# Two second-layer value steps stand inside the dense stage: one in the gate rows, one in the query rows

## The chip, the cores and the metric

The kernel runs on one core of one Trainium2 chip. The metric is the device time of one execution in microseconds; the time of a kernel is the median of several executions. The engines are written as in the profile: PE is TensorE (PEld its weight loads), DVE is VectorE, ACT is ScalarE, SP is SyncE, whose queue issues every DMA of this kernel.

## What is computed

Decoding of one token for a batch of 4, through two layers that share their weights and caches. Each layer is an attention block over a cache of 4096 positions (32 query heads, 8 key heads of 128) and a gated feed-forward block (512 to 1792 and back). All inputs are bf16.

```python
def _A_ref(x, k_cache, v_cache, wq, wo):      # x (4, 1, 512), caches (4, 8, 4096, 128)
    q = (x @ wq) split into 32 heads of 128
    k, v = each of the 8 cached heads, for 4 query heads
    p = softmax(q @ k.T * 128 ** -0.5)
    return (p @ v, heads joined) @ wo

def _B_ref(x, w_gate, w_up, w_down):
    return (gelu(x @ w_gate) * (x @ w_up)) @ w_down

x = A_x
x = x + _A_ref(layernorm(x), ...)
x = x + _B_ref(layernorm(x), ...)
x = x + _A_ref(layernorm(x), ...)             # the second layer: same weights, same caches
x = x + _B_ref(layernorm(x), ...)
```

## The kernel before

The weights are loaded once and stay on the core. The key and value caches do not fit, so they are streamed, batch by batch, as tiles of 128 x 2048 bf16 (512 KB): 16 key tiles and 16 value tiles for one batch (8 heads, each in 2 halves). Because the second layer of batch b needs the same keys as its first layer, the kernel works on two things at once: the first layer of batch b + 1 and the second layer of batch b. The keys of a batch stay in their 16 tiles until both layers have used them. The values are streamed twice, once for each layer, through 7 buffers (`KV_BUFS`).

The order of all instructions is written out by hand, one stream for each engine, and each engine takes its own in program order. So does SP's queue: a load that has to wait for its buffer holds back every load behind it.

**A value step** (`Values.step`, L467) takes one value tile: 16 weight loads and 16 matmuls of 4 columns on PE (L481). After it, its buffer is free and the next value load is put on SP (`load_v`, L454 to L461). After every second head, that is every fourth step, DVE scales the finished pair by the inverse softmax sum and writes it as bf16 (L489); the last two heads of a batch are scaled one by one, after steps 14 and 16.

**Where the second layer's steps stand.** A batch has 16 of them. Four are done early, inside `attend`. The other 12 are handed to the next pass of the main loop (L679) as `fill`: `fill(n)` takes the next n steps, if any are left. In the pass of batch b the main loop runs

- `dense(b, 1, ...)` (L660), the feed-forward block of the first layer for one row: the end of the output projection, the sums for the layer norm (`ln_center`), the gate rows (`ffn_in`, L300, matmuls at L314), the up rows (L314 again), then `ln_rstd` (L183 to L202, ten small DVE instructions that make the inverse deviation), `gelu` (which first turns the gate rows on DVE, L215), `gate_up` (which turns the up rows and ends with `H_bf`, L340) and `down` (L347);
- the second layer's query: `ln_square`, `ln_center`, the query rows of the first group of heads (`q_rows`, L218, matmuls at L225), `ln_rstd`, `am` (L690), the turn of the query rows, `q_spread` (L236), `q_build` (L246 and L249, which writes `qb`);
- `attend` (L498), or `attend_last` (L618) for the last batch: scores of the second layer against the old keys (L383), after which the key tiles are free and the keys of the next batch are loaded into them (L365); in `attend_last` they take values instead. `fill` is passed on as `rest` and called with 1 after the scores of the first group and their `q_build`, with 1 again after their softmax exponentials, and with all that is left a little later. Then come the first layer's attention for the next batch, key tiles turned on DVE as they land (L372), scores, softmax, 16 first-layer value steps and the output projection.

`seen["hold"]` keeps first-layer value loads off SP from the start of `attend` until the key loads have been issued.

Before the change, the 12 steps stand like this: one after `out_proj_end`, one after `ln_center`, one between gate and up rows, two after the GELU is issued, one after `ln_square`, one after the second `ln_center`, two after `q_spread`, one after `q_build`, and two inside `attend` or `attend_last`. In the first pass of the loop there are none, since the second layer hasn't begun (`prev` is None), and the dense stage of all four rows at the end (L705) has none either.

## Time and profile before

| | |
|---|---|
| median of 7 runs | 317.94 us (316.8 to 320.58) |
| the profiled execution | 314.99 us |
| its span | 313.2 us, 8714 instructions |
| PE, PEld busy | 212.1 us (68%), 122.3 us (39%) |
| DVE, ACT busy | 171.4 us (55%), 28.9 us (9%) |
| DMA | 114.09 MB, 364 GB/s over the span |
| value steps: matmuls (L481, values from `v`) | 1920, 63.7 us |
| key turns on DVE (L372) | 64, 75.2 us |
| gate rows, up rows (L314) | 64 and 64 matmuls, 6.7 us each |

The span runs from the first to the last instruction of the program on the core; the execution's time includes what lies around it. Busy time is an average over stages with different limits, so what a change in one stage is worth has to be read from that stage: what ends its waits, and whether what comes after it is waiting too. In the timeline a line has the start, the duration, the engine, the line of the kernel, the operation and the tiles it writes and reads; a bracket at its end tells how long the engine stood idle before it, and what ended that. In the chain of waits a line has the start, the duration and the engine or transfer that the end of the program goes back to.

### The profile page before, as it was taken

Reading aid. Unit: us, or ns where it says so; the run is one execution under the profiler, and the core shown is the slowest. Engines: PE = TensorE matmul, PEld = TensorE weight load, DVE = VectorE, ACT = ScalarE, POOL = GpSimd, SP = SyncE. Lnnn points to the kernel's source line nnn. Section 1 sums busy time; section 2 is a strip of 40 time slices with the busy share of each in tenths; the row PEclk is TensorE's granted clock in tenths of the full one; section 3 lists DMA queues with packets and bytes.
Section 4 is the critical chain, followed back from the end, with each engine's and each line's share of the span. In section 5 each row is a group of like instructions: output and inputs, shape, how many; then the busy total and the mean of one; then the engine's idle time right before and its main releaser. Section 6 shows DMA issues by size and latency. Waiting matters only on the chain.

```text
span 313.2 us, 8714 instructions
## 1 busy us (share of the span) xinstructions
PE 212.1 (68%) x3844; PEld 122.3 (39%) x3844; DVE 171.4 (55%) x481; ACT 28.9 (9%) x70; POOL 0.7 (0%) x6
## 2 busy tenths in 40 slices
PE   1360485343577649989965469799762798997975
PEld 0010245211324124656441336564411465645654
DVE  5584761014247986455488934454799553545133
ACT  0002002000002020300010112000202040003000
POOL 0000000000000000000000000000000000000000
PEclk9999999999999555555765555556755555559555
DMA  7999999999949999999999999999999999999900
GB/s 256 368 413 397 409 409 406 356 371 393 384 151 337 402 407 408 386 393 408 395 397 409 409 406 383 396 404 362 363 413 407 410 406 359 397 406 408 378 5 3
DMA packets 35526, 114.09 MB, mean 364 GB/s; under 512 B 3224, under 2 KB 9120, under 8 KB 35488
## 3 DMA queue, kind: packets, MB, share of 16 engines
q1 hardware_dynamic: 35488, 113.53, 94.3%
q8 instruction: 30, 0.49, 0.6%
q14 instruction: 8, 0.07, 0.1%
HBM read 113.51 MB, written 0.00 MB: 362 GB/s over the span
## 4 chain that ended last, share of the span: by engine, by line
DMA 44%; PE 27%; DVE 15%; SPq 9%; issue 3%; ACT 2%; DVEq 0%; ACTq 0%
DMA kt<-in_A_k_cache_dram 22%; DMA v<-in_A_v_cache_dram 18%; PE ot L481 6%; PE sc L383 6%; DVE kt L372 5%; PE rows L280 3%; DMA wd_sb<-in_B_w_down_dram 3%; PE rows L314 3%; SPq L133 3%; SPq L127 3%; PE y L347 2%; PE rows L225 2%; PE x L429 1%; DVE pp L410 1%; DVE rows L215 1%
## 5 line engine op out<-in xcount | busy, mean ns | idle before, releaser
L481 PEld LDWEIGHTS <-v 128*128 128x128 bf16 x1920 | 59.8, 105 | 47.4 <-DMA v<-in_A_v_cache_dram 23.9
L372 DVE STREAM_TRANSPOSE kt<-kt 128x1024 f32<-128x1024 f32 x64 | 75.2, 1217 | 4.7 <-DMA kt<-in_A_k_cache_dram 4.5
L481 PE MATMUL ot<-pe,v 128*128 128x4 bf16 x1920 | 63.7, 167 | 18.4 <-DMA v<-in_A_v_cache_dram 17.1
L383 PE MATMUL sc<-kt,qb 128*32 128x512 bf16 x512 | 62.9, 545 | 15.6 <-DVE kt L372 12.4
L215 DVE STREAM_TRANSPOSE rows<-rows 128x512 f32<-128x512 f32 (+1 forms) x23 | 16.3, 707 | 38.9 <-PE rows L225 19.7
L383 PEld LDWEIGHTS <-qb 128*32 128x32 bf16 x512 | 17.3, 116 | 45.8 <-issue 29.9
L402 ACT ACTIVATE pp<-sc,nm 128x512 bf16<-128x512 f32 x16 | 11.0, 688 | 152.9 <-DVE junk L398 152.9
L429 PE MATMUL x<-pp,ident_bf 128*32 128x128 bf16 x256 | 9.1, 283 | 23.5 <-DVE pp L410 23.3
L489 DVE TENSOR_TENSOR OT_bf<-ot,rden 128x8 bf16<-128x8 f32 (+1 forms) x40 | 6.5, 164 | 33.4 <-PE ot L481 32.9
L280 PE MATMUL rows<-wo_sb,OT_bf 128*1 128x512 bf16 (+1 forms) x136 | 17.2, 611 | 7.4 <-DMA wo_sb<-in_A_wo_dram 6.3
L225 PE MATMUL rows<-wq_sb,xn_bf 128*1 128x512 bf16 (+1 forms) x160 | 18.5, 612 | 4.8 <-DMA wq_sb<-in_A_wq_dram 4.5
L429 PEld LDWEIGHTS <-ident_bf 128*32 128x32 bf16 x256 | 6.7, 121 | 29.6 <-issue 27.9
L389 DVE TENSOR_REDUCE m<-sc 128x1 f32<-128x512 f32 x16 | 10.8, 675 | 12.2 <-PE sc L383 12.2
L410 DVE STREAM_TRANSPOSE pp<-pp 128x512 bf16<-128x512 bf16 x16 | 11.2, 701 | 4.6 <-ACT pp L402 4.3
L432 ACT CAST pe<-x 128x512 bf16<-128x512 f32 x16 | 9.4, 585 | 21.5 <-PE x L429 21.5
L347 PE MATMUL y<-H_bf,wd_sb 128*128 128x1 bf16 (+1 forms) x280 | 8.6, 166 | 3.0 <-DMA wd_sb<-in_B_w_down_dram 2.3
L347 PEld LDWEIGHTS <-wd_sb 128*128 128x128 bf16 x280 | 8.1, 104 | 4.3 <-DMA wd_sb<-in_B_w_down_dram 3.3
L249 DVE TENSOR_TENSOR qb<-qe,amask 128x256 bf16<-128x256 f32 x16 | 6.8, 425 | 5.3 <-PE qe L246 5.3
L225 PEld LDWEIGHTS <-xn_bf 128*1 128x1 bf16 (+1 forms) x160 | 4.4, 110 | 13.2 <-issue 11.9
L246 PE MATMUL qe<-qm,t_bf 128*128 128x64 bf16 x16 | 3.4, 215 | 8.9 <-DVE qm L236 6.6
L415 PE MATMUL den<-zx,mean_f 128*128 128x16 f32 x32 | 8.9, 357 | 0.0
L420 DVE RECIPROCAL rden<-den 128x16 f32<-128x16 f32 x16 | 4.0, 250 | 8.8 <-PE den L415 8.3
(78 smaller groups left out, 124.8 us busy)
## 6 DMA issues: line engine op xcount, KB each, us to landing
v<-in_A_v_cache_dram SPq DMA_DIRECT2D x118, 512.0 KB, 8.3
kt<-in_A_k_cache_dram SPq DMA_DIRECT2D x64, 512.0 KB, 10.6
wq_sb<-in_A_wq_dram SPq DMA_DIRECT2D x2, 2048.0 KB, 7.8
wo_sb<-in_A_wo_dram SPq DMA_DIRECT2D x4, 1024.0 KB, 11.8
kt<-in_A_v_cache_dram SPq DMA_DIRECT2D x8, 512.0 KB, 8.7
wg_sb<-in_B_w_gate_dram SPq DMA_DIRECT2D x1, 1792.0 KB, 13.5
wu_sb<-in_B_w_up_dram SPq DMA_DIRECT2D x1, 1792.0 KB
wd_sb<-in_B_w_down_dram SPq DMA_DIRECT2D x1, 896.0 KB, 16.4
```

Of the source, the lines that this page charges most:

```text
L215: nc.vector.transpose(out=rows[:, :n], in_=rows[:, :n])
L225: nc.tensor.matmul(rows[j * QS:j * QS + nb, :], lhsT=xn_bf[:, k, bs], rhs=w, start=(k == 0), stop=(k == KD - 1))
L280: nc.tensor.matmul(rows[r0:r0 + lhsT.shape[-1], :], lhsT=lhsT, rhs=wo_sb[:, i, :], start=(start and n < QD), stop=(stop and n >= hp - QD))
L347: nc.tensor.matmul(y[:, k], lhsT=wd_sb[:, c, k * P:(k + 1) * P], rhs=H_bf[:, c, :], start=(c == 0 and k == 0), stop=(c == KF - 1), skip_gr ...
L372: nc.vector.transpose(out=words, in_=words)
L383: nc.tensor.matmul(sc[s * QS:(s + 1) * QS], lhsT=qb[:, w0:w0 + 2 * W], rhs=kt[:, :, be // 2, :, be % 2], start=(t == 0 and be == 0), stop= ...
L389: nc.vector.tensor_reduce(out=m[:], in_=sc.rearrange("p c j -> p (c j)"), axis=AX.X, op=ALU.max)
L402: nc.scalar.activation(out=pp[:], in_=sc[:], func=ACT.Exp, bias=nm[:, 0:1], scale=scale, accum_out=ls[:])
L410: nc.vector.transpose(out=flat, in_=flat)
L429: nc.tensor.matmul(x[a * QS:(a + 1) * QS, s], lhsT=ident_bf[:, s * QS:(s + 1) * QS], rhs=pT[:, a], start=True, stop=True, skip_group_check ...
L432: nc.scalar.copy(out=pe.rearrange("p s c h -> p (s c h)"), in_=x.rearrange("p s t c h -> p (s t c h)"))
L481: nc.tensor.matmul(self.ot[:, s % 2], lhsT=v[:, i, :], rhs=pe[:, s, c, :], start=(c == 0), stop=(c == C - 1), skip_group_check=True)
```

## The change

`ffn_in` and `q_rows` take one more argument, a function that is called halfway through their loop over the four parts of the contraction. The dense stage passes a value step for the gate rows (not for the up rows), the main loop one for the first group's query rows.

```diff
-    def q_rows(b0, nb, g):
+    def q_rows(b0, nb, g, half=lambda: None):
         bs = slice(b0, b0 + nb)
         rows = new_rows()
         for k in range(KD):
+            if k == KD // 2:
+                half()
             for j in range(QD):
...
-    def ffn_in(b0, nb, w_sb, cols):
+    def ffn_in(b0, nb, w_sb, cols, half=lambda: None):
...
         for k in range(KD):
+            if k == KD // 2:
+                half()
             w = w_sb[:, k].rearrange("p (n a i) -> p a n i", a=QD, i=QS)
...
         fill(1)
-        rg = ffn_in(b0, nb, wg_sb, nb > 1)
+        rg = ffn_in(b0, nb, wg_sb, nb > 1, lambda: fill(1))
         fill(1)
         ru = ffn_in(b0, nb, wu_sb, nb > 1)
...
         ga, gb = groups(b + 1)
-        qr0 = q_rows(b, 1, ga)
+        qr0 = q_rows(b, 1, ga, lambda: fill(1))
```

With 12 steps in all, the 12 are now used up when `q_build` has been issued, and the calls of `rest` inside `attend` and `attend_last` find none left. The order of the steps among themselves stays.

## The prediction

> **What bounds the kernel now.** I read four views, in this order. The page's slices come first, because the first question is whether the kernel is short of data or of compute.

> ```profile
> PEclk9999999999999555555765555556755555559555
> DMA  7999999999949999999999999999999999999900
> GB/s 256 368 413 397 409 409 406 356 371 393 384 151 337 402 407 408 386 393 408 395 397 409 409 406 383 396 404 362 363 413 407 410 406 359 397 406 408 378 5 3
> ```

> A slice is 7.83 us. The DMA engines are full (about 408 GB/s) except in slice 11, where the first dense stage has no second-layer values to work on (the diff does nothing there), in the dips to 359-386, and in the last two slices, which move nothing. So most of the span is a stream of loads, with compute behind it at the end. In steady state a 512 KB tile lands every 1.274 us: the value load used at 200.05 landed at 200.00, the 16th after it at 220.38. One batch moves 48 tiles (32 values, 16 keys), so 61.2 us if the stream never thins; the first steps of the three dense stages with values start at 136.02, 200.05 and 263.68, 64.0 and 63.6 us apart.

> The chain of waits shows where the stream lets go.

> ```profile
> 256.53 8.38 DMA v<-in_A_v_cache_dram
> ...
> 264.96 0.59 PE ot L481 x16
> 265.55 1.59 PE rows L314 x16
> 267.14 0.52 PE ot L481 x16
> 267.66 1.62 PE rows L314 x16
> ...
> 270.07 0.18 DVE H_bf L340
> ...
> 270.30 1.66 PE y L347 x56
> ```

> After the tile that landed at 264.91 the chain never returns to a DMA: from 264.96 to 313.2, 48 us, it is PE and VectorE work. The third dense stage is the head of that stretch. What delays it is paid in full; what delays the first two must first use up what the stream hides.

> Third, the timeline of VectorE in that stage, since the added steps also issue VectorE work.

> ```profile
> 265.12 0.16 DVE L185 TENSOR_TENSOR msq<-mv 128x1 f32<-128x1 f32 x1
> ...
> 266.86 0.16 DVE L200 SCALAR_TENSOR_TENSOR rstd<-r,rstd 128x1 f32<-128x1 f32 x1
> 267.07 0.59 PE L481 MATMUL ot<-pe,v 128*128 128x4 bf16 x16
> 267.19 0.67 DVE L215 STREAM_TRANSPOSE rows<-rows 128x448 f32<-128x448 f32 x1 [0.18 <-PE rows L314]
> ...
> 270.16 0.17 DVE L489 TENSOR_TENSOR OT_bf<-ot,rden 128x8 bf16<-128x8 f32 x1
> ```

> The ten small operations of the inverse deviation (265.12 to 267.02) run under the gate matmuls and are done just as the rows are. The scaling of a finished pair of heads (L489) stands behind the whole GELU, at 270.16, where nobody needs VectorE.

> **The change, part by part.** A value step is 16 weight loads and matmuls, after every second head a scaling (L489) on VectorE, and one value load on SP into the buffer it frees. Twelve such steps are left when a dense stage begins. Before, ten stand in it and two in the attention that follows (282.34 and 285.02 in the last batch); now all twelve stand in the dense stage, in the same order. No step is added.

> PE, gate rows: a step between gate and up rows moves the chain by 0.52 us (267.14 to 267.66), so a step halfway through the gate rows costs 0.52 us, if its tile is there. Gate rows start at 265.48, half of their 1.59 us is 0.8, so it wants its tile at 266.28; at 1.274 us after 264.91 the tile lands at 266.19. Just in time.

> VectorE, gate rows: this is the term that the diff hides. Counting from four steps done before the stage, pairs finish at 8, 12, 14 and 16. Step 8 was the first of the two after the up rows; now it is the one between gate and up rows. Its scaling is issued there, and VectorE takes instructions in program order: in the changed kernel's instruction order L489 stands directly ahead of msq. So the ten operations, and the row turn behind them, wait for a matmul group that comes after all gate rows. In numbers of the last batch: gate rows end at 267.07 + 0.52 = 267.59, the fourth step starts; L489 follows a step's start by 0.63 (298.30 to 298.93), so 268.22; msq at about 268.42 instead of 265.12; ten operations later the first turn starts at 268.42 + 1.93 = 270.35 instead of 267.19, 3.16 late. The second turn, which waited 0.62 us for the up rows (start 269.31), can start only when the first GELU part is through: 1.50 us after the first turn (267.19 to 268.69), 271.85. That is 2.56 late, and H_bf, the down matmuls and all behind them are 2.56 late. This includes the 0.52 of PE. Queued behind the waiting L489 are msq to rstd, both turns and H_bf; PE waits for them at L347.

> Query rows: step 12 now ends just before them, so its scaling stands ahead of the second inverse deviation: 272.93 + 2.56 + 0.63 = 276.12, 0.17 long, where msq would have begun at 276.00: 0.3 late, am ends at 278.47. The rows end at 275.23 + 2.56 + 0.52 = 278.31, and their turn starts 0.28 later (275.23 to 275.51), 278.59. So the 0.3 hides under the rows, and the step costs its 0.52. The first scores begin 2.56 + 0.52 = 3.08 late.

> Attention: of the steps taken out, the one at 282.34 ran while PE waited for qb (282.54 to 282.96) and gives nothing. The other held VectorE:

> ```profile
> 285.02 0.56 PE L481 MATMUL ot<-pe,v 128*128 128x4 bf16 x16
> ...
> 285.61 0.17 DVE L489 TENSOR_TENSOR OT_bf<-ot,rden 128x4 bf16<-128x4 f32 x1 [1.35 <-PE ot L481]
> 285.69 0.70 DVE L410 STREAM_TRANSPOSE pp<-pp 128x512 bf16<-128x512 bf16 x1
> ```

> Without it pp is turned when ScalarE is done (read-out ends 285.13), at about 285.20: 0.49 back. The last batch costs 3.08 - 0.49 = 2.59 us, with nothing behind to hide it: the last value tiles land 2.4 us and more before they are used.

> SP and the stream, first two dense stages: the two freed buffers send two value loads ahead of the sixteen key loads, 2 x 1.274 = 2.55 us of DMA work, while key tiles come free 3.08 later. In the second stage the first key was issued at 215.55 with a backlog until 220.38, 4.83 us; now 218.63 against 220.38 + 2.55 = 222.93, 4.30 us. The thinnest place is the load freed by the seventh step (now after L347, issued near 211.3, backlog to 215.28) and the next four: about 4 us. Bounds: a load issued at 279.23 with backlog to 283.06 (3.8 us) landed at 284.35, on time, so 4 us can be free; in the first stage a backlog of 4.83 lost 0.5 us at the first key (156.33 to 158.11), so 4 may lose 0.8 more, some 0.9 a stage. The other end: both extra loads fill the holes around the first keys, 0.5 us in the first stage and, in the second, 1.2. Two stages: -1.7 to +1.8. I take 0, by the row at 3.8, which is nearest to 4. Later keys cost little: the keys' turns end at 246.15 where the next scores waited for values until 248.23, 2.1 us of cover against 2.55, and the 0.5 left goes under PE's output rows. Where that cover is gone it is 0.5 us a stage, inside the bounds.

> [...]

> Clock: the granted clock is 0.5 in the dense stage and full for 6.8 us from 281.9, behind the burst of 512-column matmuls at 277.31 to 282.4. That makes 32 score matmuls 2.07 us where 16 took 1.90. Everything moves together, so I take 0; if the full clock came after them, +1.7. [...]

> **The sum.** 2.59 + 0 + 0 on the profiled span: 313.2 to 315.8. That execution took 314.99, 1.8 us of it around the span, which the change doesn't touch; the median of the runs, 317.94, is 2.95 above it. Carried over as they are, 317.94 + 2.59 = 320.5.

> **Rivals.** A: the stream refills. The stream loses 64.0 - 61.2 and 63.6 - 61.2, 5.2 us in two stages. If two more loads ahead of the keys won back over 2.6 of it, the kernel is not slower; with all of it, 317.94 + 2.59 - 5.2 = 315.3. For it: the dips stand at these places. Against: the loads behind L347 come later than before, and part of the dips lie at the attention's end (slices 24 and 33), where nothing changes. With 1.7 won it is 318.8, within 0.5%.
> B: the stream thins, 0.9 a stage, or the clock misses the scores: 322.2 to 324.0. For it: five loads in a row with 4 us of backlog.
> C: the half step waits for its tile. The margin is 0.09 us; a tile late by one interval adds 1.27 in the last stage: 321.8.
> D: the change doesn't do what it says: L489 waits for nothing, and only PE's steps count: 2 x 0.52 - 0.49 = +0.55, 318.5. Against: the order on VectorE.

> **How the numbers follow.** Forecast 0.60, B 0.15, C 0.08, D 0.03, A 0.14 (0.04 below -0.5%, 0.02 between that and no change, 0.08 at 318 to 319.5). A measurement here tells 0.5% (1.6 us) from no change. Slower: 0.60 + 0.15 + 0.08 = 0.83, less 0.02 for noise; same 0.15; faster 0.04. Range: 320.5 - 1.7 - 0.5 = 318.3, to 320.5 + 1.8 and half the clock's 1.7, 323.2.

> **What would show it.** L489 ahead of msq in each dense stage with values, idle for about 3 us before it; PE idle some 2.6 us before L347; scores 3.1 us later after the stage's second step; the last stretch, from that step to the end, 2.6 longer. The first two batches apart by 63 to 65 us as before. Wrong, if that distance falls below 62.5 or PE shows no idle time before L347.

## The result and the profile after

The changed kernel takes 319.13 us in the median (317.12 to 325.66, 22 runs) against 316.8 (313.58 to 322.48, 57 runs) for the kernel before. The ratio is 1.0081, with a 95% interval of 1.0058 to 1.0104: slower, by 2.6 us (1.8 to 3.3). Medians and ranges are of all runs; ratios and their intervals leave out the runs that lie more than 1.5% above the fastest of their kernel. The forecast was 1.0081 (320.5 over 317.94).

The profiled execution has a span of 317.7 us, against 313.2. That is 4.5 us, more than the runs differ by: the 313.2 belongs to an execution of 314.99 us, 1.8 under the median of its kernel. So I compare stretches inside the traces, not whole spans, and leave whole times to the runs.

The first view is VectorE's timeline in the last dense stage of the changed kernel (lines behind the change are 2 to 4 higher: L493 is the scaling that was L489, L344 is H_bf).

```profile
270.45 0.18 DVE L493 TENSOR_TENSOR OT_bf<-ot,rden 128x8 bf16<-128x8 f32 x1 [3.28 <-PE ot L485]
270.53 0.15 DVE L185 TENSOR_TENSOR msq<-mv 128x1 f32<-128x1 f32 x1
...
272.26 0.16 DVE L200 SCALAR_TENSOR_TENSOR rstd<-r,rstd 128x1 f32<-128x1 f32 x1
272.34 0.66 DVE L215 STREAM_TRANSPOSE rows<-rows 128x448 f32<-128x448 f32 x1
...
273.74 0.66 DVE L215 STREAM_TRANSPOSE rows<-rows 128x448 f32<-128x448 f32 x1
...
274.50 0.17 DVE L344 TENSOR_TENSOR H_bf<-rows,sq 128x14 bf16<-128x14 f32 x1
274.73 1.66 PE L351 MATMUL y<-H_bf,wd_sb 128*128 128x1 bf16 x56 [1.66 <-DVE H_bf L344]
```

VectorE stands idle for 3.28 us, and what it waits for is a value step's matmuls. Only then do the ten operations of the inverse deviation run, which needed nothing from that step. The gate rows had ended at 269.89. PE in turn is idle for 1.66 us before the down matmuls.

The chain of waits of the changed kernel, in its longest pieces, shows the same place, the query rows cut in two, and the attention of the first pass that has second-layer values.

```profile
170.38 1.25 DVE kt L376
171.65 1.26 DVE kt L376
172.94 1.88 PE sc L387 x11
...
267.09 0.59 PE ot L485 x16
267.68 0.85 PE rows L318 x8
268.52 0.52 PE ot L485 x16
269.04 0.85 PE rows L318 x8
269.89 0.53 PE ot L485 x16
...
272.42 0.59 DVE rows L215
...
277.92 0.95 PE rows L227 x8
278.88 0.52 PE ot L485 x16
279.40 0.98 PE rows L227 x8
```

The half step in the gate rows took its place as soon as the first half was through and lasted 0.52, without waiting for its tile. The two halves take 0.85 each, where the rows took 1.59 in one piece, so the half step costs the chain about 0.62. At 170.38 the chain now passes through the turning of keys on VectorE, in a stretch (165.76 to 187.75) where that of the kernel before had only landings.

The last pass in numbers, from the start of its second value step (264.96 before, 267.09 after), which waits for its tile in both kernels. The 13th value step is the first of the last batch's own second layer, behind the 12 that were left:

| | before | after |
|---|---|---|
| to H_bf | 5.11 us | 7.41 us |
| to the first scores | 12.35 us | 15.59 us |
| from the first scores to the 13th value step | 10.23 us | 9.31 us |
| from the 13th value step to the end | 25.67 us | 25.70 us |
| second value step to the end | 48.26 us | 50.60 us |

2.34 us of the change lie in this stretch.

### The profile page after: what moved, and what is told of

It reads as the page before. It is cut to its first block, busy times and chain, and to the rows that moved or that the text cites. A ratio compares the mean times of both kernels' runs of the same rounds, so it can differ in the third digit from the quotient of the medians.

```text
span 317.7 us, 8718 instructions
## 1 busy us (share of the span) xinstructions
PE 214.7 (68%) x3844; PEld 121.9 (38%) x3844; DVE 171.0 (54%) x481; ACT 29.2 (9%) x70; POOL 0.7 (0%) x6
## 4 chain that ended last, share of the span: by engine, by line
DMA 31%; PE 28%; DVE 26%; SPq 8%; issue 4%; ACT 2%; DVEq 0%; ACTq 0%
DMA kt<-in_A_k_cache_dram 14%; DMA v<-in_A_v_cache_dram 14%; DVE kt L376 12%; PE ot L485 8%; PE sc L387 6%; DMA wd_sb<-in_B_w_down_dram 3%; SPq L127 3%; PE rows L227 3%; SPq L133 3%; PE rows L282 3%; PE y L351 2%; DVE rows L215 2%; PE x L433 2%; DVE pp L414 2%; DVE qb L251 1%
## 5 line engine op out<-in xcount | busy, mean ns | idle before, releaser
L387 PE MATMUL sc<-kt,qb 128*32 128x512 bf16 x512 | 64.9, 541 | 19.6 <-DVE kt L376 12.6
L485 PE MATMUL ot<-pe,v 128*128 128x4 bf16 x1920 | 63.0, 167 | 11.4 <-DMA v<-in_A_v_cache_dram 8.4
L387 PEld LDWEIGHTS <-qb 128*32 128x32 bf16 x512 | 17.8, 113 | 51.2 <-issue 34.0
L215 DVE STREAM_TRANSPOSE rows<-rows 128x512 f32<-128x512 f32 (+1 forms) x23 | 16.2, 706 | 37.1 <-PE rows L227 20.2
L493 DVE TENSOR_TENSOR OT_bf<-ot,rden 128x8 bf16<-128x8 f32 (+1 forms) x40 | 6.5, 162 | 35.4 <-PE ot L485 34.4
L248 PE MATMUL qe<-qm,t_bf 128*128 128x64 bf16 x16 | 3.4, 212 | 9.3 <-DVE qm L238 5.7
L334 ACT ACTIVATE sq<-sq 128x14 f32<-128x14 f32 (+1 forms) x5 | 1.1, 222 | 83.8 <-DVE sq L332 83.8
L318 PE MATMUL rows<-wg_sb,xn_bf 128*1 128x448 bf16 x64 | 7.2, 559 | 2.4 <-DMA wg_sb<-in_B_w_gate_dram 2.4
## 6 DMA issues: line engine op xcount, KB each, us to landing
wg_sb<-in_B_w_gate_dram SPq DMA_DIRECT2D x1, 1792.0 KB, 13.5
```

The costliest lines, as they stand in the source:

```text
L215: nc.vector.transpose(out=rows[:, :n], in_=rows[:, :n])
L387: nc.tensor.matmul(sc[s * QS:(s + 1) * QS], lhsT=qb[:, w0:w0 + 2 * W], rhs=kt[:, :, be // 2, :, be % 2], start=(t == 0 and be == 0), stop= ...
L485: nc.tensor.matmul(self.ot[:, s % 2], lhsT=v[:, i, :], rhs=pe[:, s, c, :], start=(c == 0), stop=(c == C - 1), skip_group_check=True)
```

## The experiments

**Which passes pay.** The half steps were made to depend on the pass, once for the first two passes that have second-layer values, once for the last.

```diff
+        half = (lambda: fill(1)) if b < B - 1 else (lambda: None)     # or: if b == B - 1
-        dense(b, 1, proj, fill)
+        dense(b, 1, proj, fill, half)
...
+        qr0 = q_rows(b, 1, ga, half)
```

> The two half steps stand only in the first two passes that have second-layer values; the last pass is as before. Theory (the stream of loads hides what the dense stage loses there, and the cost is paid in the last 48 us): within 0.5 us of the kernel before (ratio 0.998 to 1.002). Rival (the two extra value loads ahead of the keys make the key turns late, and the first two passes pay): 1.6 + 0.8 = 2.4 us as the two single traces show it, ratio 1.0075.

> The two half steps stand only in the last pass. Theory: nearly the whole cost of the change, 2.4 to 2.6 us, ratio 1.008; the distance from the last pass's second value step to the end grows from 48.2 to 50.6 us, the two distances between the dense stages stay as before. Rival (the first two passes pay): 0 to 0.5 us, ratio 1.000 to 1.0015.

Measured: first two passes alone 1.0033 (0.9995 to 1.0072), last pass alone 1.0124 (1.0065 to 1.0182). In the second the last stretch is 51.23 us, 2.97 longer than before, with H_bf at 7.41 and scores at 15.58, as in the changed kernel. Its two distances between dense stages, where its code is the kernel before's, are 65.73 and 64.61 us against 64.03 and 63.63: one trace's distances differ from another's by 1 to 1.7 us with no change of code there. Both were run again.

> The half steps in the first two passes alone, again, since the interval of the first time (0.9995 to 1.0072) holds both 0 and 2.3 us. Theory: ratio 1.000 to 1.002. Rival (late keys in the first two passes): 1.005 to 1.0075. About 1.003 again would say that the first two passes pay some 1 us between them.

> The half steps in the last pass alone, again, on the same chip as the run before this one. Theory: the last stretch is 2.3 to 3.0 us longer than before (by the phase of the full clock), ratio 1.007 to 1.0095. Rival: 1.000 to 1.003.

Measured: 1.0049 (1.0011 to 1.0087) and 1.0125 (1.0081 to 1.017), the second more than the 1.0095 that was expected at most; its last stretch is 51.25 us. The last pass carries most of the cost, and the rival that lets the first two passes pay alone falls. But they are not free: the two runs say 1.0 and 1.6 us, and the second interval leaves out 0. The parts, about 1.3 and 3.9 us, add up to 5.2, twice what both together cost (2.6, 1.8 to 3.3). About 0.65 of that is the last stretch, 51.2 there and 50.6 in the changed kernel (below, the clock). The rest stays open.

**Whether it is VectorE's order.** With all steps where the change puts them, the scaling of the pair finished between gate and up rows was issued after H_bf, and that of the pair finished ahead of the query rows after qm, which `q_spread` writes.

```diff
+                    if late["on"]:
+                        late["todo"].append(scale)       # scale(): the L493 of this pair
+                    else:
+                        scale()
...
         H_bf = gate_up(nb, sq, h, ru)
+        scale_late()
         fill(2)
```

> All value steps stand as in the changed kernel, but the scaling of the pair that is finished between gate and up rows is issued on VectorE after H_bf, and that of the pair finished ahead of the query rows after qm. Theory (VectorE's program order costs 2.0 of the 2.56 us): PE idle before the down matmuls falls from 1.66 us to about nothing, the last stretch is 0.52 + 0.52 - 0.5 to 0.9 = 0.1 to 0.5 us longer than before, ratio 1.000 to 1.003. Rival (the steps and their loads cost it, wherever the scaling stands): ratio 1.008 as with the changed kernel.

VectorE's timeline of the last pass in that kernel:

```profile
269.30 0.16 DVE L200 SCALAR_TENSOR_TENSOR rstd<-r,rstd 128x1 f32<-128x1 f32 x1
...
270.28 0.67 DVE L215 STREAM_TRANSPOSE rows<-rows 128x448 f32<-128x448 f32 x1 [0.82 <-PE rows L318]
...
273.15 0.17 DVE L344 TENSOR_TENSOR H_bf<-rows,sq 128x14 bf16<-128x14 f32 x1
273.24 0.17 DVE L494 TENSOR_TENSOR OT_bf<-ot,rden 128x8 bf16<-128x8 f32 x1
```

The ten operations are under the gate rows again, and H_bf comes 5.72 us after the second step: 0.61 over before, which is the half step on PE, and 1.69 less than with the change. So 1.69 of the 2.30 is the place of one instruction of 0.17 us. But the ratio is 1.0055 (1.0019 to 1.0091), more than expected, and the last stretch 49.21 instead of 48.4 to 48.8: scores come at 13.99, 0.6 later than two half steps of 0.52 explain, 0.4 with the 0.61 measured here. The run with a tile for each of the last two heads, below, tells why.

**The same order without half steps.** In the kernel before, one step was moved from behind the up rows to ahead of them.

```diff
-        fill(1)
+        fill(2)
         ru = ffn_in(b0, nb, wu_sb, nb > 1)
...
-        fill(2)
+        fill(1)
         add_y(b0, nb, down(nb, H_bf))
```

> The kernel before, with no half steps; two value steps between gate and up rows and one after the up rows, in place of one and two. So PE's work and the number of steps in the dense stage are the kernel before's, but a pair is finished between gate and up rows and its scaling stands ahead of the inverse deviation. Theory: first turn 3.1 us late, H_bf 2.5 late, nothing won in the attention: 2.5 us in the last stretch, ratio 1.006 to 1.010. Rival (it is the half steps that cost): no change, ratio 0.998 to 1.002.

Measured: 1.0112 (1.0023 to 1.02). The interval rests on two runs of six and says little; the timeline of its last pass says more:

```profile
269.57 0.18 DVE L489 TENSOR_TENSOR OT_bf<-ot,rden 128x8 bf16<-128x8 f32 x1 [2.67 <-PE ot L481]
269.66 0.15 DVE L185 TENSOR_TENSOR msq<-mv 128x1 f32<-128x1 f32 x1
...
273.85 1.30 PE L347 MATMUL y<-H_bf,wd_sb 128*128 128x1 bf16 x43 [2.20 <-DVE H_bf L340]
```

No half step, as many steps in the dense stage as before, and yet VectorE and PE stand idle in the same places, for 2.67 and 2.20 us. H_bf comes at 7.19, 2.08 late, and the last stretch is 50.33 us, 2.07 longer. At most 0.41 of the 2.08 is the step that now stands ahead of the up rows (they start 3.04 us after the second step instead of 2.63). A pair finished ahead of the inverse deviation is enough.

**Each half step alone.**

> Only the half step in the gate rows; eleven steps in the dense stage, one left in the attention. Read from the trace's last pass, from its second value step on. Theory: H_bf 2.3 us later than before (7.4 after that step instead of 5.1), scores 14.8 to 14.9 after it instead of 12.35 (0.2 to 0.3 more, because the scaling of step 12 now holds the second inverse deviation and no half step covers it), attention 0.5 shorter: last stretch 48.3 + 2.0 = 50.3 us. Rival (only PE's added steps count): H_bf 0.55 later, scores 12.9, last stretch 48.3 us.

> Only the half step in the query rows. It finishes a pair, so its scaling stands ahead of the second inverse deviation and waits for half of the query rows. Theory: H_bf as before (5.1), scores 14.1 after the second step instead of 12.35, attention 0.5 shorter, last stretch 48.3 + 1.25 = 49.5 us. Rival (only PE's added steps count): scores 12.9, last stretch 48.3 us.

Measured in the last pass, gate rows only: H_bf 7.41, scores 14.81, stretch 49.91 (expected 50.3). Query rows only: H_bf 5.11, scores 13.67, stretch 49.06 (expected 49.5). Both rivals named 48.3. These are single traces. The query rows' half step finishes a pair when it stands alone, and its scaling holds VectorE:

```profile
277.11 1.02 PE L227 MATMUL rows<-wq_sb,xn_bf 128*1 128x512 bf16 x8
277.22 0.18 DVE L493 TENSOR_TENSOR OT_bf<-ot,rden 128x8 bf16<-128x8 f32 x1 [1.59 <-PE ot L485]
277.30 0.15 DVE L185 TENSOR_TENSOR msq<-mv 128x1 f32<-128x1 f32 x1
...
279.22 0.23 DVE L694 TENSOR_SCALAR am<-amask,rstd 128x4 f32<-128x4 f32 x1
```

The same wait in a second place, 1.59 us, behind half of the query rows. With the half step it cost 1.32 here, where 1.75 was expected. Part of that is the clock: from 271.86 to 275.27 it was full in this trace, and the way from H_bf to the query rows took 3.04 us instead of 3.35. In the first of its passes with half steps, where the clock stayed at 0.50, the scores came 1.64 later than before. The attention up to the 13th step was shorter in both, by 0.8 and 0.5.

**The order mended, and a second wait.** The changed kernel with both inverse deviations issued ahead of the step that finishes a pair:

```diff
+        rstd = ln_rstd(nb, mv)
         fill(1)
         rg = ffn_in(b0, nb, wg_sb, nb > 1, lambda: fill(1))
...
-        sq, h = gelu(nb, rg, ln_rstd(nb, mv))
+        sq, h = gelu(nb, rg, rstd)
```

> The changed kernel, but both inverse deviations are issued on VectorE ahead of the value step that finishes a pair; the scaling stands where the change puts it, behind them. Theory: H_bf 5.7 us after the second step (5.1 before, 7.4 with the change), scores 14.0, last stretch 49.0 to 49.3 us. Rival (the wait is VectorE's for the matmul group whatever is queued behind it): H_bf 7.4, last stretch 50.6.

H_bf 5.80, scores 13.97, last stretch 48.99, as expected; the scaling still waits 1.42 us in VectorE's queue, but in front of the row turn alone. What is left is on PE, after the query rows of that kernel:

```profile
278.45 0.59 PE L485 MATMUL ot<-pe,v 128*128 128x4 bf16 x16
279.69 0.56 PE L485 MATMUL ot<-pe,v 128*128 128x4 bf16 x16 [0.65 <-DVE OT_bf L493]
280.11 0.21 PE L248 MATMUL qe<-qm,t_bf 128*128 128x64 bf16 x1
```

The two steps behind the query rows are now steps 14 and 15. Step 14 is scaled at once, behind qm on VectorE; step 15 writes the other half of the same accumulator tile and waits for that scaling, and the query's expansion (L248) stands behind it on PE. In the kernel before, the two were steps 12 and 13, in two tiles. With a tile for each of the last two heads:

```diff
-                if self.n % (2 * NT) == 0:
+                if self.n % (2 * NT) == 0 or self.n == VB - NT:
                     self.ot = ps_ot.tile([P, 2, rep], FP32, name="ot", tag="ot")
```

> As the run with the inverse deviations first, and the last two heads of a batch have an accumulator tile each. Theory (in the changed kernel step 15 writes the tile whose first half the scaling of step 14 still reads, so PE waits for VectorE behind qm and the query's expansion is 0.46 us late): no PE wait on the scaling between the two steps after the query rows, scores 13.5 after the second step instead of 14.0, last stretch 48.6 to 48.8 us. Rival (the 0.46 is the half step's own): scores 14.0.

```profile
276.83 1.01 PE L485 MATMUL ot<-pe,v 128*128 128x4 bf16 x32
278.00 0.21 PE L248 MATMUL qe<-qm,t_bf 128*128 128x64 bf16 x1
```

Steps 14 and 15 run as one, scores come at 13.49, last stretch 48.68. H_bf, ahead of them, came 0.07 earlier too (5.73), so that tile was 0.41 of the 0.48; in the trace of the timed run, from H_bf to the scores, it is 0.49. Timed:

> The half steps with the inverse deviations first and a tile each for the last two heads, timed. Theory: of the change's 2.4 us in the last stretch 0.4 is left (48.7 us), ratio 1.000 to 1.003. Rival (moving two steps and their loads ahead of the keys costs the first two passes 1 us or more): 1.005 or above.

Measured: 0.9977 (0.9934 to 1.002). With both waits gone the half steps cost nothing that can be told from the kernel before; nor is it shown to be faster. The rival (1.005 or above) is outside the interval. But the interval rests on seven runs of twelve; the medians of all runs, 317.42 and 316.59, would give 1.0026, so a cost below 1 us is not excluded.

**The opposite of the change.** One step fewer in the dense stage, and two behind the turn of the probabilities in the attention.

```diff
-        fill(1)
         ru = ffn_in(b0, nb, wu_sb, nb > 1)
...
         p0 = soft(sc2[0])
-        rest(1)
         soft_turn(p0)
+        rest(2)
```

> The opposite of the change, made on the kernel before: the step between gate and up rows leaves the dense stage (nine stay), and in the attention the probabilities are turned ahead of the two steps that follow their exponentials, so those fill PE's wait for VectorE. Theory: H_bf 0.5 us earlier (4.6 after the second step), scores at 11.8, attention 0.5 shorter, last stretch 47.2 to 47.4 instead of 48.3 us, nothing in the first two passes: ratio 0.995 to 0.998. Rival (fewer steps ahead of the keys thin the stream of loads): ratio 1.000 or above.

Measured: 0.9989 (0.9951 to 1.0027), no difference that can be told; the interval decides neither for the expectation nor for the rival. H_bf (4.49) and scores (11.73) came 0.62 earlier, as expected, and the attention was 0.69 shorter; but from the 13th step to the end it took 26.55 instead of 25.67 us, and the last stretch is 47.82, not 47.2 to 47.4. Two steps there now wait for their tiles:

```profile
298.50 0.59 PE L481 MATMUL ot<-pe,v 128*128 128x4 bf16 x16 [0.40 <-DMA v<-in_A_v_cache_dram]
...
303.07 0.59 PE L481 MATMUL ot<-pe,v 128*128 128x4 bf16 x16 [0.25 <-DMA v<-in_A_v_cache_dram]
```

Steps taken later free their buffers later, and the 2.4 us of slack at the end were used up. So 0.88 of the 1.31 us won came back. A thinner stream, which the rival names, is what took them, at the end of the program and not ahead of the keys.

## Why the prediction was right

**The hidden term.** The prediction's main claim, that the scaling of a finished pair would stand ahead of the inverse deviation and hold VectorE, is shown: by the idle time, by the run that moves the scaling (H_bf from 7.41 to 5.72), by the run with that order and no half steps (7.19), and by the query rows alone. H_bf was forecast 2.56 late (2.54 by the prediction's own starts, 271.85 against 269.31) and came 2.30 late. The terms that were too large are gaps, since each operation starts before the one ahead of it has ended: msq started 0.08 after the scaling (forecast 0.20), the first turn 1.81 after msq (forecast 1.93), and the second turn 1.40 after the first (forecast 1.50, which counted the last GELU operation to its end). One term was too small: the half step moved the fourth step by 0.62, not 0.52. The idle time of PE was put at some 2.6 us, as much as H_bf is late; it was 1.66, because the half step keeps PE occupied for 0.62 of the 2.30.

**Query rows.** Forecast 0.52; it was 3.24 - 2.30 = 0.94. The rows became 0.62 longer (2.43 us with the half step, 1.81 without). Of that 0.16 came back: before, `am` stood in front of the turn of the rows, and now it is done while the rows still run. The kernel before:

```profile
275.38 0.23 DVE L690 TENSOR_SCALAR am<-amask,rstd 128x4 f32<-128x4 f32 x1
275.51 0.72 DVE L215 STREAM_TRANSPOSE rows<-rows 128x512 f32<-128x512 f32 x1
```

The changed kernel:

```profile
279.97 0.23 DVE L694 TENSOR_SCALAR am<-amask,rstd 128x4 f32<-128x4 f32 x1
...
280.40 0.73 DVE L215 STREAM_TRANSPOSE rows<-rows 128x512 f32<-128x512 f32 x1 [0.20 <-PE rows L227]
```

What the forecast missed is the tile shared by steps 14 and 15. It counted which scaling comes when, but not which steps write one tile. The runs with a tile each put it at 0.41 and 0.49, and 0.62 - 0.16 + 0.48 is the 0.94.

**Attention.** Forecast 0.49 back; it was 0.92, and 0.27 and 0.24 in the two runs with the same code in the last pass. The pp turn now waits for ScalarE, as forecast:

```profile
290.13 0.71 DVE L414 STREAM_TRANSPOSE pp<-pp 128x512 bf16<-128x512 bf16 x1 [0.91 <-ACT pp L406]
```

The rest goes with the clock. From 100 us on, each trace here has the granted clock change only at times that lie whole multiples of 3.41 us apart: it became full at 152.23, 217.08 and 281.94 in the kernel before, at 156.16, 221.01 and 285.87 in the changed one, 19 times 3.41 between neighbours, and it stayed full for 6.83 us. So it depends on where the scores fall between two such times how soon they get the full clock: 4.6 us after the first score matmul before, 3.2 in the changed kernel, 5.2 and 5.7 in the two runs of the last pass alone. The later it came, the longer the stretch from the first scores to the 13th step. With the change's order of steps it is 9.31 at 3.2, 9.55 at 4.3 (the run with the scalings late), 9.96 at 5.2 and 9.99 at 5.7; with the order of the kernel before 9.95 at 3.6, 10.04 at 4.3 (both from the runs of the first two passes alone) and 10.23 at 4.6. At 4.3 the two orders differ by 0.49, which is the forecast. The other 0.43 goes with the clock, which the prediction took as 0, with up to 1.7 the other way. In the three passes with second-layer values of the kernel before, and in those of the changed one, it came 2.6 to 4.6 us after the first score.

**The end.** 2.34 us against 2.59: of the misses of -0.26, +0.42 and -0.43 the last two cancel, and the last is the phase of the clock. With the later clock of the two runs of the last pass alone it was 2.97 and 2.99. So that the whole is right to a tenth of a per cent is partly luck.

**The stream.** The prediction gave the first two passes 0, with bounds of -1.7 to +1.8, by the row of a load issued at 279.23 that landed at 284.35 with 3.8 us ahead of it. That row is misread: the load issued at 279.23 landed at 285.62, with 5.1 us ahead of it, and the one that landed at 284.35 was issued at 277.23. So the prediction had no row that shows 4 us to be free. The changed kernel has some: of six loads issued with 4.1 to 4.4 us ahead of them, five landed on time to 0.12 us and one 0.69 late.

Run alone the first two passes cost 1.0 and 1.6 us, inside the bounds but not 0; the whole change (2.6 against 2.34 in the last stretch) leaves them 0.2. Which of the two holds when all passes are changed is not settled. What was mis-sized is in the traces: the keys were to come 2.55 later with 2.1 us of cover. In three traces without half steps in these passes (the kernel before, the last pass alone twice) the last key is turned 42.9 to 44.6 us after the second value step; in three with them (the changed kernel, the first two passes alone twice) it is 46.8 to 48.4, about 3.4 later. In the first of the two passes of the changed kernel the seventh key landed at 170.35 instead of 165.69, and from there the chain runs through the key turns and the scores behind them (its lines at 170.38 to 172.94). Yet most of this is covered: the distances between dense stages are 63.6 to 65.7 us without and 64.0 to 66.4 with, 64.6 and 64.9 in the mean.

**Rivals.** A (the stream refills): the first two passes run alone won nothing. The distances between stages, 65.6 and 64.5 us where 63 to 65 were forecast, can't tell, since they reach 65.7 with the code of the kernel before. B (it thins by 0.9 a stage) is not excluded at the size of 1 to 1.6 for both. C (the half step waits for its tile) did not occur in any last pass. In the first two passes it did: in four of the 16 dense stages of the eight traces that have the half step in the gate rows there, for 0.19 to 1.38 us, as here in the second run of the first two passes alone:

```profile
203.26 0.58 PE L485 MATMUL ot<-pe,v 128*128 128x4 bf16 x16 [1.01 <-DMA v<-in_A_v_cache_dram]
```

D falls with VectorE's idle time.

## What to carry to other kernels

A unit of work that is moved takes along whatever it issues on every engine. Look where its small instruction on another engine lands in that engine's program order, and what stands behind it: here one instruction of 0.17 us, 18 places earlier, cost 1.7 us. Count also which of the moved units write one tile, for a reader between them ties the second to the first, for 0.41 and 0.49 us here. And price such a move in the stretch that nothing hides, from a landmark inside the trace, because whole times of one kernel differ by more than the effect of 2.6 us: those of the kernel before that its ratio counts go from 313.58 to 318.16 us.

## What was not expected of the hardware

The two distances between the dense stages add up to 127.7, 129.6 and 130.3 us in three traces with the same code there, so executions differ by 2.7 us there with no change in the kernel; what makes them differ was not looked into.
